# Half-filled key chunk of the expert attention on all 128 partitions, zeros laid by VectorE, and a new order of TensorE's work

## The chip, the cores and the metric

The kernel runs on one core of one Trainium2 chip. The core has TensorE (PE, with its weight loads shown apart as PEld), VectorE (DVE), ScalarE (ACT), GpSimd (POOL) and SyncE (SP), which here issues all the transfers. The metric is the device time of one execution in microseconds. Before the change the median of 3 runs is 1217.35 us (1216.65 to 1217.42).

## The reference, cut to what matters

Two layers follow each other. The first is attention of 8 batches with 8 heads each: queries are pooled in pairs (1152 become 576), keys and values stay 1152 long.

```python
q_pool = q.reshape(B, H, S // factor, factor, D).mean(axis=3)
scores = scale * np.matmul(q_pool, k.transpose(0, 1, 3, 2))
attn = np.exp(scores - max); attn = attn / (attn.sum(-1) + 1e-09)
attn_out = np.matmul(attn, v)                    # 8 x 8 x 576 x 64
```

The second is a layer of 4 experts over the 576 rows of each batch (512 wide). Each expert is a causal attention with a head of 64; a gate picks two experts for each row and weighs them.

```python
logits = x @ w_gate; topk = the 2 largest; w = softmax over the 2
for e in range(E):
    q, k, v = x @ wq[e], x @ wk[e], x @ wv[e]
    scores = np.where(causal, -1000000000.0, scale * (q @ k.transpose(0, 2, 1)))
    a = softmax(scores); ye = a @ v @ wo[e]
    out += (rows that chose e) * w * ye
```

## The kernel before

**Tiles.** Two heads of the first layer make a pair, and there are 32 pairs (4 in each batch). Scores are kept transposed, keys on partitions and queries in columns, in chunks of 128 keys; the 576 queries are cut into a block of 256 and one of 320. For each chunk PE makes the scores of both heads (line 325, three products of split operands and one that adds the row maximum), ACT turns them into exponentials in a tile `pt` of 128 x 2 x 320 (line 666), PE multiplies `pt` by the values into an accumulator (line 332, `pt,v`), and POOL adds `pt` onto a running sum `sacc` (line 349). At the end of a block PE multiplies `sacc` by ones (line 332, `sacc,ones`) to get the denominators, and DVE and ACT normalise. Row maxima come from separate products of queries and keys (line 325, `kh,qh`), which DVE reduces (line 572, `PM`).

**The experts.** After the four pairs of a batch, the expert layer of that batch runs in the same way, two experts at a time (`ep` 0 and 1), while the pairs of the next batch go on beside it. Its 576 keys make four chunks of 128 and one of 64. Chunk 4, the half chunk, meets only the last 64 queries of the block of 320. In it the scores, the exponentials (line 996), the causal mask by POOL (line 1014, an affine select) and POOL's sum (line 1046 by way of line 349) cover partitions 0 to 63 of a tile with 128. There are 16 half chunks (8 batches, 2 values of `ep`), so 16 such masks and 16 such sums; 14 of the sums are on POOL and 2, in the last batch, on DVE.

**Values of the experts.** They lie in `v32` (128 x 5 x 260); before the values of a batch are written, partitions 64 to 127 of its fifth part are set to zero by POOL (line 845), 8 times in all.

**What sets the order.** Nothing is scheduled at run time. The program is written by a planner: every piece of work is a flow that says when its inputs are ready by the planner's own clocks, and the loop at the end takes the best flow and writes its instructions to the engines' queues, which then run in that order. The flows have three modes by the shape in which PE's array is cut: A (64 rows by 128 columns, the scores), B (128 by 64, values and denominators) and C (128 by 128, projections and the rest). How long the planner stays in a mode, how many `pt` tiles it lets pile up and how it ranks row maxima and expert work is read from a table of 65 rows, one for each half of a pair: `HEAD` (16 rows), `CYCLE` (8 rows, used 5 times) and `TAIL` (9 rows). The five passes through `CYCLE` make the same order each time. The last batch of experts has nothing beside it and makes the end of the program.

A buffer is handed on through semaphores: who writes into a `pt` tile that was used before waits for the engines that read it last (PE and POOL).

Of the kernel before, what the change touches and what calls it, by code (L numbers as in the profile page):

```python
# [10 lines left out]
ALU = mybir.AluOpType  # L11
# [66 lines left out]
]  # L78
CYCLE = [
# [8 lines left out]
]  # L88
TAIL = [
# [71 lines left out]
def pooled_attention_then_moe_kernel(ctx: ExitStack, tc: tile.TileContext, qT, kT, vP, wall, wop, out):  # L161
    nc = tc.nc
# [146 lines left out]
    def pe_cost(n, m=128):  # L309
        return max(0.00086 * m, n * 0.000455 + 0.002)  # L310
# [24 lines left out]
    def act_copy(o, i, n, R, W, psum=True):  # L335
        nc.scalar.copy(o, i)  # L336
        emit("ACT", n / 1200 + (0.05 if psum else 0.083), R, W)
# [61 lines left out]
    def on(cond, *t):  # L399
        return max((0.0,) + t) if cond else INF  # L400
# [394 lines left out]
    def x_ready(b, halves):  # L795
        ps = range(b * NHP, b * NHP + NHP)
        if any(("x", p, h) not in flag for p in ps for h in halves):
            return INF
        return max(XR[p][h].rw for p in ps for h in halves)
# [37 lines left out]
    def f_vproj(b, pt):  # L837
        ts = ((0, 1), (2, 3, 4))[pt] if b == NB - 1 else range(5)
        for t in ts:
            n = min(128, SQ - 128 * t)  # L840
            hv = (0,) if t < 2 else (1,)
            yield (lambda: on("W" in flag, x_ready(b, hv), r_gen.avail(), r_v32.avail() if t == 0 else 0.0), "C")
            if t == 0:
                v32 = r_v32.new()
                nc.gpsimd.memset(v32[64:128, 4, :], 0.0)
                emit("POOL", 0.3, [], [v32])
                VG[b] = v32
            v32 = VG[b]
            ps = r_gen.new()
            xw(b, hv, ps[:n, :260], ps, lambda x, xi, W, hp: (x[:, xi, 128 * t:128 * t + n], W[:, hp, 512:772]),  # L850
               pe_cost(260))
            VT[b, t] = Res(None)
            act_copy(v32[:n, t, :], ps[:n, :260], 260, [ps], [v32, VT[b, t]])
            ps.free()
            flag.add(("v", b, t))
# [10 lines left out]
        ge, df, g, h = part(0, 16), part(16, 16), part(32, 4), part(36, 8)  # L866
        sq = lambda ap: ap.rearrange("p t (e f) -> p t e f", e=E)
        cm = [128, nt, E, E]

        def op(eng, f, *a, n=20, **kw):  # L870
# [34 lines left out]
           n=16 * nt)  # L905
# [62 lines left out]
    def f_mst(b, ep, pt):  # L968
        (qh, ql), (kh, kl) = MT[b, ep], MT[b, 2 + ep]
        rm = MRM[ep]  # L970
        tail = b == NB - 1
        for qb in ((pt,) if tail else (0, 1)):
            q0, qn = QB[qb]
            cl = (q0 + qn - 1) // 128

            span = lambda c: (max(0, 128 * c - q0), min(max(0, 128 * c - q0), qn - 128))
            for g in packed(range(cl + 1), lambda c: qn - span(c)[1]):
                yield (lambda: on(("mr", b, ep, pt) in flag and (("v", b, g[-1]) if tail else ("g", b, 0)) in flag
                                  and min(lows.get((b, m), 0) for m in (ep, 2 + ep)) > (pt if tail else 1),
                                  r_pt.avail(len(g)), r_gen.avail(2), kl.rw, ql.rw, rm.rw), "A")  # L980
                pts, st, o = [r_pt.new() for _ in g], [r_gen.new() for _ in range(2)], 0
                at = []
                for c in g:
                    kn, (f, w) = min(128, SQ - 128 * c), span(c)
                    kc, qc = slice(128 * c, 128 * c + kn), slice(q0 + w, q0 + qn)
                    rows2(lambda j: st[j][:kn, o:o + qn - w],
                          [(lambda r: kh[r, kc], lambda r: qh[r, qc]), (lambda r: kl[r, kc], lambda r: qh[r, qc]),
                           (lambda r: kh[r, kc], lambda r: ql[r, qc]), (lambda r: ON[r, :kn], lambda r: rm[r, qc])],
                          [kh, kl, qh, ql, rm], st)
                    o += qn - w  # L990
                    at.append(o)
                for j in range(2):
                    for c, pt_, o in zip(g, pts, at):
                        kn, f = min(128, SQ - 128 * c), span(c)[0]
                        n = qn - f
                        nc.scalar.activation(pt_[:kn, j, f:qn], st[j][:kn, o - n:o], AF.Exp, scale=0.125)
                        emit("ACT", n / 1200 + 0.06, [st[j]], [pt_], late=0.05)
                    st[j].free()
                for c, pt_ in zip(g, pts):
                    m_prog[b] += 0.48  # L1000
                    if 128 * c >= q0:
                        spawn("mask", f_mask(b, ep, qb, c, pt_, span(c)[0], min(128, SQ - 128 * c)))
                    else:
                        spawn("mav", f_mav(b, ep, qb, c, pt_), av_prio)
        if q0 + qn == SQ:
            flag.add(("mst", b, ep))
            for m in (ep, 2 + ep):
                for t in MT.pop((b, m)):
                    t.free()

    def f_mask(b, ep, qb, c, pt, f, kn):
        yield lambda: pt.rw
        sq = pt[:kn, :, f:f + kn]
        nc.gpsimd.affine_select(out=sq, in_=sq, compare_op=ALU.is_ge, fill=0.0, base=0,  # L1014
                                pattern=[[0, 2], [1, kn]], channel_multiplier=-1)
        emit("POOL", 0.15 + 0.0025 * kn, [pt], [pt])
        spawn("mav", f_mav(b, ep, qb, c, pt), av_prio)

    def f_mav(b, ep, qb, c, pt):
        q0, qn = QB[qb]  # L1020
        kn = min(128, SQ - 128 * c)
        f = max(0, 128 * c - q0)
        cl = (q0 + qn - 1) // 128
        v32, vr = VG[b], VT[b, c]
# [8 lines left out]
        acc, sacc = ACC[key], SACC[key]  # L1033
        n = qn - f
# [3 lines left out]
        if c == 0:  # L1038
            act_first(sacc[:, :, :qn], pt[:, :, :qn], 2 * qn, [pt], [sacc])
        else:  # L1040
            add = any_tt if tail_now() else pool_tt
            add(sacc[:kn, :, f:qn], sacc[:kn, :, f:qn], pt[:kn, :, f:qn], ALU.add, 2 * n, [pt], [sacc])
        pt.free()
        m_prog[b] += n * 0.0017
        if c == cl:
# [102 lines left out]
    while flows:  # L1148
# [16 lines left out]
        key, f, need = best  # L1165
# [31 lines left out]
```

## Time and profile before

| | |
|---|---|
| median of 3 runs | 1217.35 us |
| the profiled execution | 1215.55 us, of which its span 1213.8 us |
| PE busy | 1160.3 us (96% of the span) |
| POOL busy | 971.6 us (80%) |
| DVE busy | 877.6 us (72%) |
| ACT busy | 703.8 us (58%) |
| granted clock of TensorE | 0.996 |

The span runs from the first to the last instruction of the profiled execution; 1.75 us of its time lie outside it. Busy is the time in which an engine had an instruction under way; a PE that is shown busy is not always at its peak, since the ends of matmuls are modelled. A wait names the engine whose instruction came last before the waiting engine went on.

### The profile page before, as it was taken

How to read it: one execution, taken by the hardware profiler on the slowest of the kernel's cores; microseconds unless marked ns; L12 is line 12 of the kernel's file. 1: busy time of each engine (PE TensorE's matmuls, PEld its weight loads, DVE VectorE, ACT ScalarE, POOL GpSimd, SP SyncE). 2: the span in 40 equal slices, each digit the busy share in tenths (PEclk: the TensorE clock that was granted, in tenths of full speed). 3: DMA queues.
4: the chain of work that ended last, by engine and by line, in shares of the span. 5: the costliest groups of instructions: out<-in, count | busy, mean ns of one | idle time of the engine just before them, and what ended most of it. 6: DMA issues, size and time to landing. Idle time of an engine off the chain costs nothing.

```text
span 1213.8 us, 29441 instructions
## 1 busy us (share of the span) xinstructions
PE 1160.3 (96%) x11233; PEld 893.0 (74%) x11233; DVE 877.6 (72%) x2091; ACT 703.8 (58%) x2036; POOL 971.6 (80%) x850
## 2 busy tenths in 40 slices
PE   6999999999999999989999999998999989999998
PEld 5676786778767787667786677876877668877785
DVE  7897668776777857777677876777767876677265
ACT  5676446665466564665556654566546666465634
POOL 4999979887699866998669887698786986879921
PEclk9999999999999999999999999999999999999999
DMA  4232212031112211122011221112211122110001
GB/s 156 80 101 69 60 53 67 10 106 41 60 53 63 78 49 41 54 68 93 22 41 54 83 85 37 32 47 84 77 41 34 53 71 87 42 33 9 1 36 44
DMA packets 40425, 70.30 MB, mean 58 GB/s; under 512 B 4870, under 2 KB 31452, under 8 KB 40284
## 3 DMA queue, kind: packets, MB, share of 16 engines
q1 hardware_dynamic: 40284, 68.43, 18.2%
q8 instruction: 88, 1.44, 0.5%
q14 instruction: 53, 0.43, 0.1%
HBM read 58.73 MB, written 9.44 MB: 56 GB/s over the span
## 4 chain that ended last, share of the span: by engine, by line
PE 57%; POOL 29%; DVE 8%; issue 2%; ACT 2%; DMA 0%; POOLq 0%; SPq 0%; DVEq 0%; ACTq 0%
POOL sacc L349 25%; PE gen L325 23%; PE gen L316 17%; PE gen L332 16%; DVE qraw L345 3%; POOL kl L349 3%; POOL pt L1014 2%; DVE PM L572 1%; DVE gen L956 1%; ACT pt L666 1%; DVE ql L345 1%; PE gen L622 0%; DMA qraw<-in_qT 0%; DVE gen L734 0%; DVE gen L345 0%
## 5 line engine op out<-in xcount | busy, mean ns | idle before, releaser
L349 POOL TENSOR_TENSOR sacc<-sacc,pt 128x640 f32<-128x640 f32 (+4 forms) x586 | 824.8, 1412 | 138.2 <-ACT sacc L341 101.8
L572 DVE TENSOR_REDUCE PM<-gen 128x1 f32<-128x384 f32 x864 | 426.1, 550 | 164.1 <-PE gen L325 132.9
L666 ACT ACTIVATE pt<-gen 128x320 f32<-128x320 f32 (+1 forms) x1152 | 381.5, 433 | 142.9 <-PE gen L325 133.3
L332 PE MATMUL gen<-pt,v 128*64 128x320 f32 (+4 forms) x2752 | 354.8, 401 | 1.2
L332 PEld LDWEIGHTS gen<-pt,v 128*64 128x64 f32 (+1 forms) x2752 | 191.7, 137 | 136.8 <-issue 11.3
L325 PE MATMUL gen<-qh,kh 64*128 64x320 f32 (+1 forms) x1152 | 211.4, 317 | 13.4 <-DVE PM L572 10.9
L325 PE MATMUL gen<-qh,kl 64*128 64x320 f32 (+1 forms) x1152 | 196.0, 297 | 0.0
L325 PE MATMUL gen<-RM,ON 64*128 64x320 f32 (+1 forms) x1152 | 191.9, 293 | 0.8 <-ACT RM L336 0.8
L325 PE MATMUL gen<-ql,kh 64*128 64x320 f32 (+1 forms) x1152 | 191.3, 293 | 0.0
L325 PEld LDWEIGHTS gen<-qh,kh 64*128 64x128 f32 x1152 | 132.7, 186 | 45.8 <-DVE PM L572 18.6
L325 PE MATMUL gen<-kh,qh 64*128 64x384 f32 x768 | 156.8, 369 | 7.8 <-ACT qh L336 6.9
L325 PEld LDWEIGHTS gen<-RM,ON 64*128 64x128 f32 x1152 | 130.4, 187 | 1.2 <-ACT RM L336 1.0
L325 PEld LDWEIGHTS gen<-ql,kh 64*128 64x128 f32 x1152 | 129.7, 187 | 0.0
L325 PEld LDWEIGHTS gen<-qh,kl 64*128 64x128 f32 x1152 | 127.4, 187 | 0.0
L325 PEld LDWEIGHTS gen<-kh,qh 64*128 64x128 f32 x768 | 88.3, 188 | 38.5 <-issue 17.6
L316 PE MATMUL gen<-x,WH 128*128 128x320 f32 (+1 forms) x512 | 104.9, 299 | 6.8 <-DVE x L345 6.8
L349 POOL TENSOR_TENSOR kl<-kraw,kh 128x384 fp32r<-128x384 f32 x96 | 96.1, 1019 | 10.2 <-ACT mqh L336 5.2
L956 DVE CUSTOM_DVE_ANT_0 gen<-gen,mqk 64x288 f32<-64x288 f32 (+4 forms) x160 | 74.5, 504 | 23.8 <-PE gen L325 21.3
L316 PEld LDWEIGHTS gen<-x,WH 128*128 128x128 f32 x512 | 82.1, 188 | 10.0 <-issue 8.1
L332 PE MATMUL gen<-sacc,ones 128*64 128x320 f32 (+1 forms) x384 | 66.7, 428 | 14.5 <-POOL sacc L349 14.0
L316 PE MATMUL gen<-x,WL 128*128 128x320 f32 (+1 forms) x256 | 75.5, 295 | 0.0
L722 DVE STREAM_TRANSPOSE rd<-gen 128x256 f32<-128x256 f32 (+1 forms) x96 | 45.6, 475 | 41.3 <-PE gen L332 40.8
(115 smaller groups left out, 1575.6 us busy)
## 6 DMA issues: line engine op xcount, KB each, us to landing
kraw<-in_kT SPq DMA_DIRECT2D x96, 192.0 KB
v<-in_vP SPq DMA_DIRECT2D x96, 192.0 KB
qraw<-in_qT SPq DMA_DIRECT2D x31, 576.0 KB
out<-ob SPq DMA_DIRECT2D x28, 256.0 KB
wst<-in_wall SPq DMA_DIRECT2D x8, 193.0 KB
out<-pt SPq DMA_DIRECT2D x4, 256.0 KB
RM<-nt SPq DMA_DIRECT2D x62, 2.5 KB
out<-ob SPq DMA_DIRECT2D x6, 128.0 KB
```

The source lines that it names most:

```text
L316: nc.tensor.matmul(o, lhsT, rhs, start=start, stop=stop)
L325: nc.tensor.matmul(o(j), l(HEAD[j]), r(HEAD[j]), start=i == 0, stop=i == len(terms) - 1)
L332: nc.tensor.matmul(o(HEAD[j]), l(j), r(j), start=start, stop=stop)
L345: nc.vector.tensor_tensor(o, a, b, op=op)
L349: nc.gpsimd.tensor_tensor(o, a, b, op=op)
L572: nc.vector.tensor_reduce(pm[:, i, t:t + 1], ps[:, :384], axis=AX.X, op=ALU.max)
L666: nc.scalar.activation(pts[i][:, j, :qn], st[j][:, qn * i:qn * i + qn], AF.Exp, scale=0.0625)
L722: nc.vector.transpose(rd[:, :n], den[:, :n])
L956: nc.vector.tensor_tensor_reduce(p, p, mqk[:m, 384 + m - w:384 + m], 1.0, LOW, ALU.add, ALU.max, pm[:m, j, c, i:i + 1])
L1014: nc.gpsimd.affine_select(out=sq, in_=sq, compare_op=ALU.is_ge, fill=0.0, base=0, pattern=[[0, 2], [1, kn]], channel_multiplier=-1)
```

## The change

Three things are edited.

- The mask of a half chunk and the sum of every chunk name all 128 partitions. For the half chunk, VectorE first sets partitions 64 to 127 of the 64 columns to zero; this memset is written to its queue when the scores of the group are, before ScalarE's exponentials.
- The memset of `v32` goes from POOL to VectorE.
- In the planner's table four rows of `HEAD` and one of `TAIL` have other numbers. The order comes out otherwise in four places of PE's queue, and the same everywhere else: about 116 to 134 us, 188 to 294 us, 1030 to 1053 us and 1177 us to the end by the times of the profile before. Between 294 and 1030 us the queues of PE, ACT and SP are the same instruction by instruction, and those of POOL and DVE are the same apart from the first two edits. PE has the same matmuls before and after; it changes its mode 329 times before and 322 times after, 3 fewer between 188 and 294 us and 4 fewer behind 1177 us.

```diff
-    (0.2, 0.1, 0.2, 1, 4, 0.7, 0.12, 0.02, 2, 4.5, 3.9, 4.05, 4.1),
+    (0.2, 0.1, 0.2, 1, 4, 0.7, 0.25, 0.02, 2, 4.5, 3.9, 4.05, 4.75),
...
         if t == 0:
             v32 = r_v32.new()
-            nc.gpsimd.memset(v32[64:128, 4, :], 0.0)
-            emit("POOL", 0.3, [], [v32])
+            nc.vector.memset(v32[64:128, 4, :], 0.0)
+            emit("DVE", 0.3, [], [v32])
...
             pts, st, o = [r_pt.new() for _ in g], [r_gen.new() for _ in range(2)], 0
+            if g[-1] == 4:
+                nc.vector.memset(pts[-1][64:128, :, qn - 64:qn], 0.0)
+                emit("DVE", 0.13, [], [pts[-1]])
...
 def f_mask(b, ep, qb, c, pt, f, kn):
     yield lambda: pt.rw
-    sq = pt[:kn, :, f:f + kn]
+
+    sq = pt[:, :, f:f + kn]
...
-        add(sacc[:kn, :, f:qn], sacc[:kn, :, f:qn], pt[:kn, :, f:qn], ALU.add, 2 * n, [pt], [sacc])
+        add(sacc[:, :, f:qn], sacc[:, :, f:qn], pt[:, :, f:qn], ALU.add, 2 * n, [pt], [sacc])
```

DVE's queue in the first pass through `CYCLE`, at about 347 us (`ql` is the low part of a pair's queries, the ISA rows are the experts' row maxima). Before:

```order
L572 TENSOR_REDUCE PM_99<-gen_5614 128x1
L345 TENSOR_TENSOR ql_5632<-qraw_5042,qh_5109 128x576
L956 ISA gen_5686,MPM_103<-gen_5686,mqk 128x512
L956 ISA MPM_103 128x1
L956 ISA gen_5687,MPM_103<-gen_5687,mqk 128x512
```

The same place after:

```order
L572 TENSOR_REDUCE PM_99<-gen_5616 128x1
L345 TENSOR_TENSOR ql_5634<-qraw_5044,qh_5111 128x576
L983 MEMSET pt_5675 64x2x64
L956 ISA gen_5689,MPM_103<-gen_5689,mqk 128x512
L956 ISA MPM_103 128x1
```

One memset has come in between the subtraction and the row maxima; it waits for POOL's sum that read this `pt` tile last.

PE's queue at the end of the program, around the last denominators (`sacc,ones` is the denominators of the last block, `OH` and `OL` the output weights, `y_18932` or `y_18935` the first and `y_19049` or `y_19090` the second pair of experts). Before:

```order
L316 MATMUL gen_18989<-OH,y_19049 128x512 x2
L316 MATMUL gen_18989<-OL,y_19049 128x512
L332 MATMUL gen_19095<-pt_19115,v_8_18720 64x320 x2
L332 MATMUL gen_19095<-pt_19116,v_8_18720 64x192 x2
L332 MATMUL gen_19095<-pt_19152,v_8_18720 64x64 x2
L316 MATMUL gen_19186<-OH,y_18932 128x512 x2
L316 MATMUL gen_19186<-OL,y_18932 128x512
L316 MATMUL gen_19186<-OH,y_19049 128x512 x2
L316 MATMUL gen_19186<-OL,y_19049 128x512
L332 MATMUL gen_19198<-sacc_19096,ones 64x320 x2
L316 MATMUL gen_19202<-OH,y_18932 128x512 x2
L316 MATMUL gen_19202<-OL,y_18932 128x512
```

The same place after:

```order
L332 MATMUL gen_19109<-pt_19120,v_8_18734 64x320 x2
L332 MATMUL gen_19109<-pt_19121,v_8_18734 64x192 x2
L332 MATMUL gen_19109<-pt_19155,v_8_18734 64x64 x2
L316 MATMUL gen_19188<-OH,y_18935 128x512 x2
L316 MATMUL gen_19188<-OL,y_18935 128x512
L316 MATMUL gen_19188<-OH,y_19090 128x512 x2
L316 MATMUL gen_19188<-OL,y_19090 128x512
L316 MATMUL gen_19202<-OH,y_18935 128x512 x2
L316 MATMUL gen_19202<-OL,y_18935 128x512
L332 MATMUL gen_19207<-sacc_19110,ones 64x320 x2
L316 MATMUL gen_19202<-OH,y_19090 128x512 x2
L316 MATMUL gen_19202<-OL,y_19090 128x512
```

There are ten output products (an `OH` row and an `OL` row) in the queue's end. Before, four stand ahead of the last denominators (one of them further up) and six behind; after, three stand ahead and seven behind. The last three, which need what comes of these denominators, are the end of the queue in both. On DVE's queue the last whole chunk's addition to these denominators' `sacc` (line 345, 128 x 640) stands ahead of three instructions that normalise the block before (lines 731, 734 and 345), and before the change behind them.

PE's queue in the first expert layer, at about 189 us, where the row maxima of the experts (`mkh,mqh`) end. Before:

```order
L325 MATMUL gen_3038<-mkh_2179,mqh_2161 64x288
L316 MATMUL gen_3045<-kh_2580,QD_101 128x384
L316 MATMUL gen_3048<-kh_2732,QD_101 128x384
L622 MATMUL gen_3051<-ident,nm_3012 9x128
L332 MATMUL gen_3055<-sacc_2735,ones 64x256 x2
L332 MATMUL gen_3064<-pt_2961,v_2086 64x320 x2
```

What stands there after:

```order
L325 MATMUL gen_3159<-mkh_2432,mqh_2415 64x288
L622 MATMUL gen_3168<-ident,nm_3012 9x128
L622 MATMUL gen_3174<-ident,nm_3132 10x128
L316 MATMUL gen_3179<-gate_2864,rep 128x80
L332 MATMUL gen_3183<-sacc_2735,ones 64x256 x2
L332 MATMUL gen_3192<-pt_2961,v_2098 64x320 x2
```

The transposes (`ident`) and the gate product, which lay in two mode changes, lie in one, and the row maxima of the second pair of experts come ahead of them; behind the denominators nine products of `pt` follow without a break, where there were four.

## Rows read from the trace of the kernel before

**Rows 1.** The page: busy time and share of the span, by engine.

```profile
PE 1160.3 (96%) x11233; PEld 893.0 (74%) x11233; DVE 877.6 (72%) x2091; ACT 703.8 (58%) x2036; POOL 971.6 (80%) x850
```

**Rows 2.** Windows: stretch, length, busy us of PE, PEld, DVE, ACT, POOL; clock, DMA.

```profile
116.00:134.00 18.00, 16.59 (x169) 12.26 (x166) 11.84 (x26) 9.87 (x31) 17.14 (x13) 1.00 0.22 68
188.00:294.00 106.00, 105.09 (x1050) 79.25 (x1046) 80.23 (x190) 67.14 (x196) 91.00 (x79) 1.00 0.19 62
294.00:1030.00 736.00, 707.18 (x6944) 547.42 (x6944) 539.89 (x1255) 432.58 (x1255) 602.51 (x527) 1.00 0.19 58
1177.00:1213.80 36.80, 31.63 (x251) 21.14 (x249) 23.46 (x88) 17.36 (x52) 7.14 (x14) 0.97 0.11 37
```

**Rows 3.** Waits of PE, 294 to 1030 us: total, times, longest.

```profile
PE gen L325 <- DVE PM L572: 10.9, 5, 2.2
PE gen L332 <- POOL sacc L349: 7.2, 10, 1.0
```

**Rows 4.** Timeline of DVE, places of the first cycle and the last sum.

```profile
349.20 0.70 DVE L956 CUSTOM_DVE_ANT_0 gen<-gen,mqk 128x512 f32<-128x512 f32 x1 [0.88 <-PE gen L325]
...
382.37 0.56 DVE L572 TENSOR_REDUCE PM<-gen 128x1 f32<-128x384 f32 x1 [1.01 <-PE gen L316]
...
389.42 6.74 DVE L345 TENSOR_TENSOR qraw<-qraw 128x576 f32<-128x576 f32 x1
...
1202.41 0.28 DVE L345 TENSOR_TENSOR sacc<-sacc,pt 64x128 f32<-64x128 f32 x1 [1.19 <-POOL sacc L349]
```

**Rows 5.** Groups by shape, POOL: count, busy us, mean ns, idle before.

```profile
L1014 POOL TENSOR_SCALAR_AFFINE_SELECT pt<-pt 128x256 f32<-128x256 f32 x64 | 25.4, 418 | 32.6 <-ACT pt L996 32.6
L349 POOL TENSOR_TENSOR sacc<-sacc,pt 128x384 f32<-128x384 f32 x16 | 16.0, 998 | 3.5 <-DVE sacc L345 3.0
L349 POOL TENSOR_TENSOR sacc<-sacc,pt 128x256 f32<-128x256 f32 x16 | 12.2, 766 | 3.6 <-ACT sacc L341 3.6
L349 POOL TENSOR_TENSOR sacc<-sacc,pt 64x128 f32<-64x128 f32 x14 | 8.3, 593 | 0.9
L1014 POOL TENSOR_SCALAR_AFFINE_SELECT pt<-pt 64x128 f32<-64x128 f32 x16 | 7.3, 454 | 0.2 <-ACT pt L996 0.2
L845 POOL MEMSET v<- 64x260 f32 x8 | 2.5, 310 | 0.5
L172 POOL TENSOR_SCALAR_AFFINE_SELECT ident<-ident 128x128 f32<-128x128 f32 x1 | 0.3, 292 | 0.0
```

**Rows 6.** Line 1014 alone: shortest, median and longest ns, first and last start.

```profile
L1014 POOL TENSOR_SCALAR_AFFINE_SELECT pt<-pt x80: 285/406/936, 205.9 to 1199.7; 128x256 f32<-128x256 f32 x64, 64x128 f32<-64x128 f32 x16
```

**Rows 7.** Timeline of POOL: start, us, instructions, idle before and releaser.

```profile
360.98 0.46 POOL L349 TENSOR_TENSOR sacc<-sacc,pt 64x128 f32<-64x128 f32 x1
395.63 0.85 POOL L349 TENSOR_TENSOR sacc<-sacc,pt 64x128 f32<-64x128 f32 x1
...
437.53 3.98 POOL L349 TENSOR_TENSOR sacc<-sacc,pt 128x512 f32<-128x512 f32 x3 [9.16 <-ACT sacc L341]
```

**Rows 8.** Timeline of DVE at the program's start: a memset.

```profile
1.19 0.17 DVE L196 MEMSET ON<- 128x128 f32 x1
```

**Rows 9.** Timeline of PE, the last denominators and output products.

```profile
1202.99 0.76 PE L332 MATMUL gen<-sacc,ones 128*64 128x320 f32 x4
1203.68 0.73 PE L316 MATMUL gen<-OH,y 128*128 128x512 f32 x2
1204.25 0.40 PE L316 MATMUL gen<-OL,y 128*128 128x512 f32 x1
1204.48 0.63 PE L316 MATMUL gen<-OH,y 128*128 128x512 f32 x2
1204.95 0.40 PE L316 MATMUL gen<-OL,y 128*128 128x512 f32 x1
...
1206.45 1.07 PE L316 MATMUL gen<-OH,y 128*128 128x512 f32 x2 [0.40 <-ACT y L336]
```

**Rows 10.** Timeline of PEld: the same denominators' weights.

```profile
1202.99 0.20 PEld L332 LDWEIGHTS gen<-sacc,ones 128*64 128x64 f32 x4 [0.37 <-DVE sacc L345]
```

8 rows, old and new, of tables (HEAD, TAIL) are left out of this document.

## The prediction

> **What bounds the kernel now.** I read the page's busy line first [rows 1]: PE is busy 96% of the span, POOL 80%, DVE 72%. The reader is to see that about 53 us of PE's span are idle, and that a faster POOL or DVE pays only where PE waits for it. Then I read the busy time by stretches, cut where PE's queue differs between the two programs [rows 2]. From 294 to 1030 us, where PE, ACT and SP have the same instructions in the same order, PE has 736.00 - 707.18 = 28.8 us idle, 5.8 in each of five cycles. Between 188 and 294 us it has 0.9 idle, and behind 1177 us 5.2.
>
> Then the waits of PE in the five cycles [rows 3]: 10.9 us in five waits for DVE's `PM` and 7.2 us in ten waits for POOL's sum at the denominators. The first kind is one place in each cycle. DVE's subtraction `qraw`, which reads two operands, lasts 6.74 us there [rows 4], though 128x576 elements take a small part of that when nothing holds it, and the row maxima queue behind it. Neither edit touches that subtraction. So the bulk of the span repeats unless the edits move POOL or DVE at these waits.
>
> **The wider mask and sum.** The groups by shape [rows 5] seem to promise something. The half chunk's mask takes 454 ns on 64x128, a mask of 128x256 takes 418 and one of 128x128 (`ident`, line 172) 292. The sum takes 593 ns on 64x128; from 766 at 256 columns and 998 at 384 a sum of 128 columns would take 766 - 232 = 534. If the excess were the price of half the partitions, widening would save 16 x 0.162 + 14 x 0.059 = 3.4 us of POOL's time.
>
> The single rows say otherwise. The shortest mask of line 1014 took 285 ns [rows 6], and as none of 256 columns would be shorter than `ident`'s 292, it is one of the 64-partition ones. Two sums of one shape in one cycle took 0.46 and 0.85 us [rows 7], and the long one, at 395.63, starts while the `qraw` subtraction (389.42 + 6.74 = 396.16) is under way [rows 4]. The means are thus raised by a few instructions that stand beside a DVE instruction with two operands, and width is not the cause. I take 0 for the widening, between bounds of 3.4 us of POOL's time saved and, if a sum on all partitions were as long as the longer of the two sums, 14 x 0.39 = 5.5 us more. Even a gain would reach PE only through the ten waits for `sacc`, two in a cycle.
>
> On this the Trainium skill (GPSIMD Engine Reference, section 2 Architecture) says that each of the eight cores works on its own 16 partitions, which would leave four of them without work in a 64-partition instruction and its time unchanged; by that the saving is 0, and the single rows agree while the means do not.
>
> **The memset of v32.** POOL loses 8 x 0.31 = 2.5 us [rows 5]. In the cycles that relieves nothing: POOL sits idle 9.16 us before the sum at 437.53 [rows 7]. Taken 0; at best the 2.5 us come back.
>
> **The memsets on DVE.** There are 16 of 128 columns on 64 partitions; the nearest row, 128x128, took 0.17 us [rows 8], so 2.7 us together. The eight of `v32` (260 columns) are by size 0.17 x 260/128 = 0.35 us each, 2.8 together. Cover: they fall at places where DVE waited for PE's products anyway, 0.88 us before the row maxima at 349.20 and 1.01 before `PM` at 382.37 [rows 4]. Taken 0; all uncovered they are 5.5 us. The first adds a wait, since the memset needs a `pt` tile that POOL's sum has read. Behind it on DVE stand the experts' row maxima, for which ACT and then PE wait; but POOL's sums run earlier there than DVE arrives, by the slack that these gaps show.
>
> A memset on DVE could also be held by POOL, as `qraw` was. The Trainium skill (SBUF — State Buffer, section "Who interferes with whom") states that a DVE instruction contends with GpSimd when it reads two operands from SBUF or runs in a 2-port mode, and that whoever issues first keeps the shared ports. By it the memset, which reads nothing, is not held unless it runs in such a mode, and the sum stays as it is; the 6.74 us row agrees with the rule, and no row here shows a DVE memset beside a POOL sum.
>
> **The order of PE's work.** Between 188 and 294 us there are three mode changes fewer. A change costs little: at the end an `OH` product that follows the denominators starts its `OL` 0.57 us later (1203.68 to 1204.25), and one that follows its own kind 0.47 (1204.48 to 1204.95) [rows 9], so about 0.1 in the first product, and as much again, estimated, in leaving the old mode. 3 x 0.2 = 0.6 us. Upper bound: all of the 0.9 us idle on top, 1.5. Below nothing: new waits, rival three.
>
> In 116 to 134 us POOL is busy 17.14 of 18.00 and PE 16.59 [rows 2]; POOL paces it and its work is the same. 0, with bounds of 0.5 us either way. Between 1030 and 1053 us, where PE has the same products in another order, the same.
>
> At the tail, four mode changes fewer. Before, the last denominators start at 1202.99 and the first product that needs them at 1206.45, 3.46 us later, after 0.40 us of PE idle [rows 9]. That chain runs through DVE and ACT and is fixed. Three products filled it; after the change four do, each about 1204.48 - 1203.68 = 0.8 us at most. With one product fewer ahead of the denominators they come about 0.7 us earlier and the 0.40 us of idle closes. Against it: their weights already waited 0.37 us for DVE's sum [rows 10], and that sum (1202.41) had waited 1.19 us for POOL's [rows 4]. If the sums stayed there, the earlier denominators would gain nothing. But DVE's whole-chunk sum, for which POOL's waits, now stands ahead of three normalising instructions, so I let the sums come earlier by as much as the denominators. Taken: 0.7 for the denominators and 0.3 for what is left of the mode changes, -1.0 us. Bounds: +0.5 (the sums late) to -2.5 (all of the waits at 1202.99 to 1206.45 and four changes gone together).
>
> **The sum.** Widening 0, `v32` 0, memsets on DVE 0, mode changes -0.6, the two short stretches 0, tail -1.0: -1.6 us. The profiled execution took 1215.55 us, so 1213.95 for one like it. It lay 1.80 us under the median, which gives 1217.35 - 1.6 = 1215.75, say 1215.8. A measurement of this kernel can tell about 0.2%, 2.4 us, from no change: below 1214.9 is faster, above 1219.8 slower. The forecast is no measurable change.
>
> **Rivals.**
>
> One, POOL does get faster by the widening (means, not single rows). For: 454 against 292 ns [rows 5]. Against: 285 [rows 6]. Of the 3.4 + 2.5 us that POOL would save, the `sacc` waits could return 2.5 on top of the forecast: 1217.35 - 1.6 - 2.5 = 1213.3.
>
> Two, the order is worth more: the 0.9 us idle between 188 and 294 goes with the mode changes (-1.5), and behind 1177 us, where PE idles 5.2 us [rows 2], two more of the small waits close (-2.0). -3.5 gives 1213.8. For: the tail is a chain of short dependent steps, and moving a sum ahead of three instructions shortens each link behind it. Against: the last 3.46 us are fixed.
>
> Three, slower: in 188 to 294 us nine products of `pt` now follow the denominators without a break, so PE uses up its tiles faster than POOL, busy 91.0 of 106 us there [rows 2], adds them, and later denominators wait for the sum. The price is the longest such wait, 1.0 us [rows 3], at each. Up to four of them are eaten by the other gains (4.0 - 1.6 = 2.4); five and more decide: six give 1217.35 - 1.6 + 6.0 = 1221.8. Against: PE has 0.9 us idle there, and the stretch ends with the same queue as before.
>
> Four, slower: POOL's sums hold the DVE memsets. One of 998 ns [rows 5] makes a memset 1.17 us, 0.29 beyond the 0.88 of cover; at 16 places 4.6 us, so 1220.4. It decides when the holding exceeds the cover by 0.25 us at each. For: `qraw`'s 6.74 us [rows 4]; against: that one reads two operands.
>
> **How the numbers follow.** Forecast 0.48, rival one 0.08, two 0.25, three 0.12, four 0.07. Of the forecast's own range, 1214.7 to 1217.5, a small part (0.03) lies under 1214.9. Faster is 0.08 + 0.25 + 0.03 = 0.36, slower 0.12 + 0.07 = 0.19, the same 0.45. The range runs from 1212.6, under rivals one and two by the spread of the runs, to 1219.8: it leaves out the slower cases and a small part of the faster ones.
>
> **What would show it.** Right: the five cycles keep their length; POOL's masks and sums on 128 partitions have shortest rows of 0.29 and 0.46; the memsets on DVE take 0.17 and 0.35 with shorter idle ahead of what follows; the stretch that now ends at 294 us is 0.6 shorter; the last products follow the denominators with no idle. Wrong: cycles that change by over 0.3 us each, waits of PE for `sacc` in 188 to 294, memsets of 1 us, or denominators at the end that wait for DVE longer than 0.37.

## The result, and the profile after

The changed kernel takes 1204.42 us (median of 4 runs, 1204.27 to 1205.93) beside 1217.0 us of the kernel before (4 runs, 1215.95 to 1217.42): a ratio of 0.9901, 95% interval 0.9884 to 0.9918. It is 12.6 us faster, where 1.6 were forecast and the range ended at 1212.6.

The page of the changed kernel, busy time by engine. DVE's is 17 us shorter than before [rows 1], although DVE has 22 instructions more.

```profile
PE 1158.4 (96%) x11233; PEld 892.0 (74%) x11233; DVE 860.6 (71%) x2113; ACT 704.5 (58%) x2036; POOL 972.0 (81%) x844
```

The windows of the three long stretches, cut at the places that answer to 188 to 294, 294 to 1030 and 1177 us to the end of before (columns as in [rows 2]).

```profile
187.20:297.20 110.00, 108.23 (x1051) 80.13 (x1049) 80.22 (x194) 67.65 (x196) 91.20 (x79) 0.97 0.19 60
297.20:1019.00 721.80, 703.44 (x6948) 545.75 (x6946) 522.07 (x1270) 432.67 (x1255) 601.59 (x521) 1.00 0.20 59
...
1166.30:1204.20 37.90, 30.97 (x251) 21.34 (x247) 23.02 (x90) 17.05 (x52) 9.69 (x16) 0.98 0.11 36
```

The five cycles, where PE, ACT and SP have the same instructions in the same order, became 14.2 us shorter (736.0 to 721.8), of which 10.5 us are idle time of PE (28.8 to 18.4); the other 3.7 are busy time of PE, nearly all of it a lower clock before, as the end of this section shows. Both long stretches with a new order became longer, by 4.0 and 1.1 us (2.3 of the 4.0 are a lower clock in this one execution, shown below). So the sign of each was the other way than forecast: what was to stay gained, and what was to gain lost. Of the two short stretches, the one around 116 to 134 us became 1.4 us shorter and the one around 1030 to 1053 us 0.5 longer.

The waits of PE in the cycles (total, times, longest). The five waits for DVE's `PM`, 10.9 us [rows 3], are gone; the ten for POOL's sum are as they were.

```profile
PE gen L332 <- POOL sacc L349: 7.2, 10, 1.0
```

Behind that wait stood the `qraw` instruction of 6.74 us [rows 4] (the prediction calls it a subtraction; it adds the two halves of the pooled queries). First POOL's timeline in the kernel before around it: the mask of the half chunk on 64 partitions, and directly behind it a train, five of POOL's instructions that follow each other without a pause. The fifth ends at 394.55 + 1.00 = 395.55. Up to its next sum, at 395.63 [rows 7], POOL pauses for 0.08 us, and there DVE gets through.

```profile
388.75 0.31 POOL L1014 TENSOR_SCALAR_AFFINE_SELECT pt<-pt 64x128 f32<-64x128 f32 x1
389.01 4.63 POOL L349 TENSOR_TENSOR sacc<-sacc,pt 128x640 f32<-128x640 f32 x3
393.59 1.01 POOL L349 TENSOR_TENSOR kl<-kraw,kh 128x384 fp32r<-128x384 f32 x1
394.55 1.00 POOL L349 TENSOR_TENSOR sacc<-sacc,pt 128x384 f32<-128x384 f32 x1
```

The same place in the changed kernel, POOL (the mask is on 128 partitions now) and DVE. DVE gets through at the first boundary of two sums: it needs 1.79 us, and three sums take 5.15 instead of 4.63, because the second waits for it. Each of the five cycles shows 1.79 or 1.80 where it had 6.74 or 6.75.

```profile
392.00 0.29 POOL L1018 TENSOR_SCALAR_AFFINE_SELECT pt<-pt 128x128 f32<-128x128 f32 x1
392.26 5.15 POOL L349 TENSOR_TENSOR sacc<-sacc,pt 128x640 f32<-128x640 f32 x3
...
392.65 1.79 DVE L345 TENSOR_TENSOR qraw<-qraw 128x576 f32<-128x576 f32 x1
```

The groups that answer to [rows 5] and to the new memsets (count, busy, mean ns, idle before). The wide mask takes what the narrow one took (455 against 454); the sum's mean fell from 593 to 457, since none is held by the late DVE instruction any more. The memsets take 165 and 275 ns.

```profile
L1018 POOL TENSOR_SCALAR_AFFINE_SELECT pt<-pt 128x128 f32<-128x128 f32 x16 | 7.3, 455 | 0.2 <-ACT pt L999 0.2
L349 POOL TENSOR_TENSOR sacc<-sacc,pt 128x128 f32<-128x128 f32 x15 | 6.9, 457 | 0.9
L983 DVE MEMSET pt<- 64x128 f32 x16 | 2.6, 165 | 1.3
L845 DVE MEMSET v<- 64x260 f32 x8 | 2.2, 275 | 0.9
```

The stalls of `qraw` had a second price before. PE waits 2.2 us behind each of the five. Behind the second one (that wait ends at 545.41) the clock was granted at 0.50, its lower level of 1.2 GHz, for 3.4 us, and so it was behind the fourth; behind the other three it stayed at its upper level. Two windows of the kernel before (the clock is the third number from the right), then its first and second cycle from one `qraw` to the next, and the same two of the changed kernel, where the clock stays up:

```profile
544.00:546.00 2.00, 0.59 (x10) 0.59 (x12) 2.00 (x4) 1.08 (x3) 1.11 (x2) 1.00 0.00 0
546.20:549.70 3.50, 3.50 (x26) 2.24 (x22) 1.99 (x5) 2.72 (x9) 0.27 (x1) 0.51 0.45 140
389.42:538.15 148.73, 142.87 (x1410) 110.68 (x1410) 109.79 (x255) 87.39 (x254) 121.58 (x107) 1.00 0.19 58
538.15:686.85 148.70, 143.24 (x1404) 110.58 (x1404) 109.29 (x255) 86.91 (x253) 121.44 (x107) 0.99 0.18 56
```

```profile
392.65:539.20 146.55, 142.62 (x1411) 110.57 (x1410) 105.64 (x257) 87.67 (x254) 121.49 (x106) 1.00 0.20 59
539.20:684.04 144.84, 141.53 (x1404) 109.75 (x1404) 106.94 (x258) 86.80 (x253) 121.37 (x106) 1.00 0.19 58
```

The first gained 2.2 us, the second 3.9, of which 1.7 are busy time of PE. Two such drops of the clock make 3.4 of the 3.7 us above.

### The profile page after: what moved, and what is told of

Same layout as the page of the kernel before. It is cut to its first block, busy times and chain, and to the rows that moved or that the text cites. A ratio compares the mean times of both kernels' runs of the same rounds, so it can differ in the third digit from the quotient of the medians.

```text
span 1204.2 us, 29456 instructions
## 1 busy us (share of the span) xinstructions
PE 1158.4 (96%) x11233; PEld 892.0 (74%) x11233; DVE 860.6 (71%) x2113; ACT 704.5 (58%) x2036; POOL 972.0 (81%) x844
## 4 chain that ended last, share of the span: by engine, by line
PE 61%; POOL 27%; DVE 5%; ACT 3%; issue 3%; DMA 1%; POOLq 0%; SPq 0%; DVEq 0%; ACTq 0%
PE gen L325 24%; POOL sacc L349 23%; PE gen L316 19%; PE gen L332 17%; POOL kl L349 3%; ACT pt L666 2%; POOL pt L1018 1%; DVE gen L956 1%; DVE PM L572 1%; DVE ql L345 1%; ACT pt L999 1%; PE gen L622 0%; DVE gen L734 0%; DMA qraw<-in_qT 0%; DVE gen L345 0%
## 5 line engine op out<-in xcount | busy, mean ns | idle before, releaser
L336 ACT CAST x<-gen 128x256 fp32r<-128x256 f32 x64 | 25.8, 403 | 86.9 <-DVE gen L345 86.8
```

## The experiments

The theory formed from the two traces: a POOL instruction on fewer than 128 partitions, directly ahead of a train of sums, keeps DVE's two-operand instruction out until the train ends; the new order, which moves the instant at which DVE meets the train, and the memset of `v32` are the rivals. Five of the kernels below (m3, m2, m1b, m6 and m8) were timed in one execution each, and there it is the durations of `qraw`, cycle by cycle, that count.

**Which edit.** Four kernels, timed together with before (1216.92 us in these rounds). The first (e1) has the order of before on every engine:

```diff
+                if g[-1] == 4:
+                    nc.vector.memset(pts[-1][64:128, :, qn - 64:qn], 0.0)
...
-        sq = pt[:kn, :, f:f + kn]
+        sq = pt[:, :, f:f + kn]
...
-            add(sacc[:kn, :, f:qn], sacc[:kn, :, f:qn], pt[:kn, :, f:qn], ALU.add, ...)
+            add(sacc[:, :, f:qn], sacc[:, :, f:qn], pt[:, :, f:qn], ALU.add, ...)
```

Expected: 

> The order of before on every engine, with the mask and the sum of the half chunk on 128 partitions and the zeros laid by DVE (v32's memset stays on POOL). Theory 1 (width: an instruction on 64 partitions leaves POOL's cores out of step, so that the ports they share with DVE are never all free between back-to-back sums): the five qraw subtractions of 6.74 us shrink to about 1.8 and the time falls by 5 x 2.2 to 5 x 2.9 us, to 1202 to 1206. Theory 2 (the new order between 188 and 294 us shifts the phase at which DVE meets POOL): the 6.74 us stay, 1216 to 1218. Theory 3 (v32's memset off POOL does it): 1216 to 1218 as well.

Measured: 1201.69 us, ratio 0.9875 (0.9858 to 0.9891), all five at 1.80 or 1.81 us. The width alone gains 15.2 us; neither the order nor `v32` is needed, and with them the kernel is 2.7 us slower than with the width alone.

The other three keep the changed kernel's order and go back to 64 partitions in both (e2), in the mask alone (e3), in the sum alone (e4):

```diff
-        sq = pt[:, :, f:f + kn]
+        sq = pt[:kn, :, f:f + kn]
...
-            add(sacc[:, :, f:qn], sacc[:, :, f:qn], pt[:, :, f:qn], ALU.add, ...)
+            add(sacc[:kn, :, f:qn], sacc[:kn, :, f:qn], pt[:kn, :, f:qn], ALU.add, ...)
```

Expected of both narrow: 

> The changed kernel, its order on every engine kept, with mask and sum back on 64 partitions (the zeros are still laid). Theory 1: the 6.74 us stalls are back in each cycle and the time is 1215 to 1220, since the order of 188 to 294 us and the tail cost what the two traces showed (+3.9 and +1.1 us). Theories 2 and 3: no stall, 1203 to 1206.

Expected of the mask alone: 

> The changed kernel with the mask alone back on 64 partitions, the sum on 128. In the trace of before the narrow mask stands directly ahead of the train of sums in which DVE was held, the narrow sum at its end. Theory 1 with the mask as the cause: stalls of about 6 us are back, 1215 to 1220. If the sum is the cause, or the phase: 1203 to 1206.

Expected of the sum alone: 

> The changed kernel with the sum alone back on 64 partitions, the mask on 128. Theory 1 with the mask as the cause: no stall over 2.1 us in DVE's qraw, 1203 to 1206. If the narrow sum is the cause: 1215 to 1220.

Measured: 1220.83 us (ratio 1.0029, 1.0016 to 1.0042), 1220.48 us (1.0026, 1.0015 to 1.0037) and 1204.42 us (0.9898, 0.9883 to 0.9912). The first two have five stalls of 6.74 to 6.77 us, the third none over 1.83. The mask's width is worth 16 us, the sum's nothing. Part of the 16 is the clock: in the profiled execution of e3 it fell to 0.50 behind three of the five stalls. With both back on 64 partitions the change is a loss of 3.9 us. Over all the kernels here, the clock fell within the five cycles behind 16 of 27 stalls of `qraw`, for 3.4 us each, and never in the seven kernels that have no stall.

**Is it the instant?** Before, with one to five DVE memsets ahead of the held instruction (m3):

```diff
+        if p in LAG:                      # {13: 1, 17: 2, 21: 3, 25: 4, 29: 5}
+            for _ in range(LAG[p]):
+                nc.vector.memset(SCR[:, :], 0.0)
         any_tt(q[:, 0, :], q[:, 0, :], q[:, 1, :], ALU.add, SQ, [q], [q])
```

Expected: 

> Before, with 1 to 5 memsets on DVE (256 columns, about 0.3 us each) ahead of the held qraw subtraction in the first to fifth cycle, so that it comes at five other phases of POOL's sums. Theory 1 (no gap in the whole train): it ends at the same place in each cycle, at the end of the train, so it takes about 6.4, 6.1, 5.8, 5.5 and 5.2 us, and the time stays at 1215 to 1218. Theory 2 (phase): it is under 2.5 us in some of the cycles.

Measured: 6.47, 6.11, 5.68, 5.30 and 4.93 us, 1216.96 us in all. Whenever it comes, it is held to the end of the train. DVE in the first and the fifth cycle:

```profile
389.39 6.47 DVE L347 TENSOR_TENSOR qraw<-qraw 128x576 f32<-128x576 f32 x1
...
987.51 4.93 DVE L347 TENSOR_TENSOR qraw<-qraw 128x576 f32<-128x576 f32 x1
```

**How narrow?** e1, with another width of the mask in each cycle (m2):

```diff
-        sq = pt[:, :, f:f + kn]
+        sq = pt[:kn if kn == 128 else {1: 64, 2: 80, 3: 96, 4: 112}.get(b, 128), :, f:f + kn]
```

Expected: 

> The order of before with the sum on 128 partitions and the mask of the half chunk on 64, 80, 96, 112 and 128 in the first to fifth cycle. Theory 1a: any core left out of the mask runs ahead, so qraw takes 5 to 7 us in cycles 1 to 4 and 1.8 us in the fifth. If only a split in two halves matters: 6.7 us in the first cycle alone. Phase (theory 2): no rule in the widths. With 4 stalls of 5 the time is about 1214, with one about 1205.

Measured: 6.75, 6.75, 6.76, 6.77 and 1.80 us, and 1213.99 us. Sixteen partitions left out do as much as 64. The fourth cycle (its narrow mask and DVE's wait) and DVE in the fifth:

```profile
834.83 0.31 POOL L1016 TENSOR_SCALAR_AFFINE_SELECT pt<-pt 112x128 f32<-112x128 f32 x1
835.50 6.77 DVE L345 TENSOR_TENSOR qraw<-qraw 128x576 f32<-128x576 f32 x1
...
984.20 1.80 DVE L345 TENSOR_TENSOR qraw<-qraw 128x576 f32<-128x576 f32 x1
```

**Why does a narrow one do it?** The guess was that the part of POOL without work runs ahead and stays ahead. The first trial (m1) adds a second narrow mask on the upper half behind the lower one, in the kernel before:

```diff
+        if kn < 128:
+            up, src = pt[kn:2 * kn, :, f:f + kn], ident[kn:2 * kn, :].rearrange("p (j c) -> p j c", j=2)
+            nc.gpsimd.affine_select(out=up, in_=src, compare_op=ALU.is_ge, fill=0.0, base=0,
+                                    pattern=[[0, 2], [1, kn]], channel_multiplier=-1)
```

Expected: 

> Before, with a second narrow mask instruction behind each narrow one, on partitions 64 to 127 of the same columns (nobody reads what it writes there; no zeros on DVE, sum on 64). Theory 1a (the narrow instruction lets the idle cores of POOL run ahead, and they stay ahead through the back-to-back sums): the second one lets the other half catch up, the five stalls of 6.74 us go and the time is 1201 to 1206. Theory 1b (each instruction on fewer partitions does the harm by itself, in whatever pair): the stalls stay, 1216 to 1220.

Measured: 1203.70 us, ratio 0.9894 (0.9879 to 0.9909). The stalls are gone, but `qraw` takes 0.75 us, so DVE did not come in within the train but before it, in a pause of 0.08 us that POOL made between the second mask and the first sum. I took the pause for a wait of the second mask for the first and tried to remove the wait, by letting it write a scratch tile (m1b, `up` in `SCR`):

Expected: 

> m1 again without its gap: in m1 the second narrow mask waited for the first, POOL had a pause of 0.08 us before the sums, and DVE's qraw got in there (0.75 us), before the train. Here the second one writes a scratch tile that nothing else uses, so it waits for nothing and the sums follow at once. Theory 1a (cores out of step; the second lets the others catch up): DVE comes in at the first boundary of two sums as in the changed kernel, 1.7 to 2.3 us in all five cycles, and the time is 1202 to 1205. Theory 1b (a narrow instruction does harm by itself): 6.7 us, 1216 to 1219. If the two halves are only nearly in step, values between.

Measured: 1203.02 us and again 0.74 or 0.75 us. The pauses are still there, 0.06 us ahead of the upper mask and 0.09 us behind it:

```profile
388.15 0.65 POOL L1015 TENSOR_SCALAR_AFFINE_SELECT pt<-pt 128x256 f32<-128x256 f32 x2
388.86 0.29 POOL L1019 TENSOR_SCALAR_AFFINE_SELECT SCR<-ident 64x128 f32<-64x128 f32 x1
389.16 0.74 DVE L346 TENSOR_TENSOR qraw<-qraw 128x576 f32<-128x576 f32 x1
389.24 2.09 POOL L350 TENSOR_TENSOR sacc<-sacc,pt 128x640 f32<-128x640 f32 x1
```

The scratch tile did not remove the wait. In the records of this trace the upper mask, and the sum behind it, wait for the semaphore that POOL's own instructions raise; the lower mask, which follows without a pause, does not. In the kernel before the same wait stands at 470 of the 472 instructions that POOL starts after a pause of 0.04 to 0.10 us. So the pauses are POOL waiting for its own earlier instruction, as the program has it; why it has it at these two, the runs do not show. This pair shows that a pause of under 0.1 us is enough to let DVE in; whether the halves catch up it cannot tell. Two more kernels (m6 and m8) put small memsets of a scratch tile between the wide mask and the train, another kind in each cycle (the second is the same with other entries):

```diff
+EXTRA = {1: [(0, 64, 8)], 2: [(0, 64, 64)], 3: [(0, 64, 256)], 4: [(0, 128, 64)], 5: [(0, 64, 64), (64, 128, 64)]}
...
+        if kn < 128 and ep == 1:
+            for lo, hi, n in EXTRA.get(b, ()):
+                nc.gpsimd.memset(SCR[lo:hi, :n], 0.0)
```

Expected of the first: 

> The order of before with mask and sum on 128 partitions (no stall in e1), and one more POOL memset of a scratch tile between the wide mask and the train of sums: 64 partitions x 8 columns in the first cycle, x 64 in the second, x 256 in the third, 128 partitions x 64 in the fourth, and 64 columns on the lower and then the upper 64 partitions in the fifth. Theory 1a: qraw takes over 5 us in cycles 1 to 3 (in the first perhaps less, if so small a lead is lost again), 1.8 in cycles 4 and 5. Theory 1b: over 5 us in 1, 2, 3 and 5. If it is the mask and not the width: 1.8 us in all. With three stalls the time is about 1211, with none 1203.

Expected of the second: 

> As m6 (wide mask and sum, one more POOL memset of a scratch tile ahead of the train), to see what the lead is made of: cycle 1 the upper 64 partitions x 64 columns alone, cycle 2 four memsets of 64 partitions x 8 columns (m6 had one, 0.10 us, and no stall), cycle 3 64 x 32, cycle 4 64 x 64 followed by one of 128 x 64, cycle 5 four of 128 x 8. Theory 1a (idle cores run ahead and keep the lead): cycle 1 stalls for 6 to 7 us as the lower half does, cycle 2 stalls (four small leads add up), cycle 3 stalls or not by where the threshold lies between 8 and 64 columns, cycle 4 stalls (a wide one behind does not give the lead back), cycle 5 has 1.8 us. If only the instruction directly ahead of the first sum counts: no stall in cycle 4, and none in cycle 2.

Measured, first kernel (1210.34 us): 1.84, 6.83, 7.02, 1.90 and 0.75 us. The memset and `qraw` in the first, second and fourth cycle:

```profile
389.68 0.10 POOL L1022 MEMSET SCR<- 64x8 f32 x1
390.10 1.84 DVE L347 TENSOR_TENSOR qraw<-qraw 128x576 f32<-128x576 f32 x1
...
535.96 0.14 POOL L1022 MEMSET SCR<- 64x64 f32 x1
536.38 6.83 DVE L347 TENSOR_TENSOR qraw<-qraw 128x576 f32<-128x576 f32 x1
...
835.22 0.17 POOL L1022 MEMSET SCR<- 128x64 f32 x1
835.64 1.90 DVE L347 TENSOR_TENSOR qraw<-qraw 128x576 f32<-128x576 f32 x1
```

Second kernel (1204.66 us): 2.10, 1.93, 1.85, 6.91 and 1.96 us. Its first and fourth cycles (the last memset row holds two, 64 x 64 and behind it 128 x 64):

```profile
388.21 0.15 POOL L1023 MEMSET SCR<- 64x64 f32 x1
388.52 2.10 DVE L348 TENSOR_TENSOR qraw<-qraw 128x576 f32<-128x576 f32 x1
...
825.50 0.25 POOL L1023 MEMSET SCR<- 64x64 f32 x2
825.92 6.91 DVE L348 TENSOR_TENSOR qraw<-qraw 128x576 f32<-128x576 f32 x1
```

What follows: the operation does not matter (mask or memset), and the width does: 64 partitions x 64 columns stall, 128 x 64 do not. A wide one behind a narrow one does not undo it (fourth cycle here, the memset of 64 x 64 and one of 128 x 64). A narrow one must be long enough: 0.10 and 0.12 us (8 and 32 columns) did nothing, 0.14 us did, and four of 8 columns did not add up, against what I expected. The upper half alone stalled nothing (2.10 us), but POOL waited for itself on both sides of that memset (0.06 and 0.09 us), as it did around the upper one of the first kernel's fifth cycle and not around the lower ones. So the upper half is not decided: its waits may have undone what it did. Whether parts of POOL run ahead cannot be seen in the trace, which has one row for the whole engine; that stays a guess, and the four small memsets speak against its simple form.

**What the order costs.** A version that takes what gained (m5): e1, with only the first changed row of the table (it rewrites 116 to 134 us), and the last batch left on 64 partitions without zeros.

```diff
-    (0.2, 0.1, 0.2, 1, 4, 0.7, 0.12, 0.02, 2, 4.5, 3.9, 4.05, 4.1),
+    (0.2, 0.1, 0.2, 1, 4, 0.7, 0.25, 0.02, 2, 4.5, 3.9, 4.05, 4.75),
...
-                if g[-1] == 4:
+                if g[-1] == 4 and b < NB - 1:
...
-        sq = pt[:, :, f:f + kn]
+        sq = pt[:kn if b == NB - 1 else 128, :, f:f + kn]
```

Expected: 

> A version meant to beat both: the order of before with only the table's first changed row (116 to 134 us), mask and sum on 128 partitions with zeros by DVE in the first seven batches, both on 64 in the last batch, v32's memset on POOL. From e1 (1201.7): -1.3 for 116 to 134 us and -1.0 for the end, where e1 showed 0.6 us of PE idle that before did not have: 1199.4, between 1198.5 and 1201.7. If the last batch's width is not what costs at the end: 1200.4.

Measured: 1199.84 us (1199.71 to 1199.98), ratio 0.9862 (0.9845 to 0.9878). It beats both kernels, the changed one by 4.6 us. Then the three rows of 188 to 294 us were put into it (m7):

```diff
-    (0.05, 0.2, 0.3, 1, 3, 1.4, 0.2, -0.02, 3, 4.05, 2.9, 4.6, 4.75),
+    (0.15, 0.1, 0.3, 1, 4, 0.9, 0.3, -0.02, 0, 4.5, 3.9, 4.6, 4.55),
...
-    (0.2, 0.1, 0.6, 3, 1, 1.2, 0.12, -0.02, 2, 4.05, 3.9, 4.05, 4.55),
+    (0.2, 0.1, 0.3, 3, 2, 1.2, 0.12, -0.04, 2, 4.05, 3.9, 4.6, 4.55),
...
-    (0.05, 0.1, 0.1, 2, 1, 1.0, 0.16, 0.04, 1, 4.5, 3.9, 4.05, 4.1),
+    (0.05, 0.1, 0.1, 2, 1, 0.9, 0.12, 0.04, 1, 4.5, 3.9, 4.05, 4.1),
```

Expected: 

> m5 with the three changed rows of the table that rewrite 188 to 294 us, everything else as in m5. The trace of the changed kernel showed PE waiting 1.2 us there for DVE's row maxima of the experts, and this stretch 1.6 to 3.9 us longer than before. Theory: the order of this stretch costs 1.5 to 3 us, so 1201.3 to 1202.9 against 1199.84 for m5. If the order is worth the 0.6 us of the prediction: 1199.2.

Measured: 1202.76 us, ratio 0.9894 (0.9877 to 0.9911): 2.9 us lost by the order of this stretch. PE waits there 1.5 us for DVE, in three places, and once for ACT, which the changed kernel does not show (total, times, longest):

```profile
PE gen L316 <- ACT QD L336: 1.2, 1, 1.2
```

The timeline of the changed kernel shows where it waits for DVE: the transposes of the experts' row maxima and the gate product, which now stand together right behind the row maxima's products, wait for DVE, which is still reducing them.

```profile
194.97 0.28 PE L622 MATMUL gen<-ident,nm 128*9 128x128 f32 x1 [0.69 <-DVE MPM L956]
...
195.74 0.38 PE L622 MATMUL gen<-ident,nm 128*10 128x128 f32 x1 [0.50 <-DVE MPM L956]
...
196.35 0.69 PE L316 MATMUL gen<-gate,rep 128*128 128x80 f32 x2 [0.23 <-DVE MPM L956]
```

That pause had a second price in the profiled execution of the changed kernel. Its windows there (the clock is the third number from the right), and then those of the kernel with the narrow sum (e4), which has the same order and the same pause, with the whole stretch of 188 to 294 us as its last row:

```profile
194.00:196.00 2.00, 0.81 (x4) 0.23 (x3) 1.93 (x10) 1.32 (x3) 0.00 (x0) 0.90 0.56 172
196.00:200.00 4.00, 3.77 (x15) 1.99 (x16) 3.92 (x16) 0.28 (x1) 3.48 (x3) 0.50 0.00 0
200.00:204.00 4.00, 4.00 (x24) 1.99 (x22) 2.01 (x5) 0.37 (x1) 3.84 (x3) 0.70 0.28 59
```

```profile
194.00:196.00 2.00, 0.59 (x3) 0.24 (x3) 1.93 (x10) 1.16 (x3) 0.10 (x1) 1.00 0.38 113
196.00:200.00 4.00, 4.00 (x28) 2.06 (x30) 3.89 (x15) 0.00 (x0) 3.84 (x3) 1.00 0.00 1
186.90:294.60 107.70, 105.55 (x1051) 78.84 (x1048) 80.50 (x195) 67.58 (x195) 91.42 (x78) 1.00 0.19 61
```

In the first, after PE had been busy for 0.81 of 2 us, the clock was granted at 0.50, its lower level of 1.2 GHz, for 4 us and came back within the next 4; the stretch took 110.0 us. In the second, after 0.59 of 2 us, it stayed at its upper level, and the stretch took 107.7: 2.3 us of the changed kernel's 4.0 are the clock, and 1.7 the order. Of the five profiled executions with this order the clock fell at this pause in three (the changed kernel, e2, e3) and not in two (e4, m7), so the pause does not bring it about each time. The changed kernel's profiled execution took 1205.93 us and its three others 1204.27 to 1204.53.

## Why the prediction was wrong

**What bounds the kernel.** The reading was right: PE is the bound, and the largest of its repeated waits is the one for `PM` behind `qraw`. The step that failed is the one drawn from it, "Neither edit touches that subtraction", and with it "the bulk of the span repeats". The mask one instruction ahead of the train did touch it (e3 and e4: 1220.48 against 1204.42 us). I had named the 6.74 us as a case of two operands beside POOL and left it at that. The trace of before had more: 31 such `qraw` instructions, of which five took 6.74 or 6.75 us and no other more than 2.02. What those five had in front of them on POOL, a 64-partition mask directly ahead of the train, was the question to ask. The cycles, which were to keep their length, each became shorter by 2.1 us or more.

**The wider mask and sum.** The cost on POOL itself came out as taken: 455 ns for 454, and the two long kinds of row were indeed those beside a DVE instruction. But I bounded the edit by POOL's own time alone, between 3.4 us saved and 5.5 lost, and by what of it would reach PE through `sacc`. Its effect lay on another engine, and no bound covered it. The conclusion drawn beside the Trainium skill's rule (GPSIMD Engine Reference, section 2 Architecture: each core works on its own 16 partitions) was wrong in the same way: a narrow mask does take as long as a wide one (454 and 455 ns), and the edit was worth far more than the 0 that was concluded from it. The Trainium skill's rule in SBUF — State Buffer, section "Who interferes with whom", that whoever issues first gets the shared ports for the whole instruction, does not account for the five rows, although the prediction read them as agreeing with it: behind a narrow instruction DVE was kept out over five POOL instructions, 6.74 us, and only behind wide ones did it come in at the end of one.

**v32 and DVE's memsets.** Both taken at 0. The memsets took 165 and 275 ns (0.17 and 0.35 were taken); none was held (all 16 took 165 ns, all eight 275), so rival four fell. What the move of `v32` alone is worth was not tried.

**The order, 188 to 294 us.** Forecast -0.6, measured +2.9 (m7 against m5, 1.2 of it in the wait for ACT that only m7 has); by the trace of e4 +1.7, at the upper clock. The step that failed is pricing a regrouping by the mode changes it saves, without asking what the regrouped instructions wait for; the transposes that now stand first at that place need DVE's row maxima, which are produced just before. Rival three had the sign, at +2.4 and more, by another mechanism: PE waited for DVE, not for POOL's sums.

**116 to 134 us and the tail.** The first was put at 0, within 0.5 us either way, since POOL paced it. It gained 1.4 us. Between the same two products, before and after:

```profile
108.10:140.00 31.90, 29.14 (x274) 22.26 (x275) 18.73 (x41) 17.16 (x49) 30.59 (x23) 1.00 0.18 57
108.70:139.20 30.50, 28.66 (x274) 21.99 (x275) 19.47 (x41) 17.27 (x49) 29.32 (x22) 1.00 0.20 59
```

The reading that POOL's work there is the same did not hold for the time it takes: 1.3 us less of POOL's busy time falls into the stretch, and PE idles 0.9 us less. In the tail, the end came as described: three products, the denominators, and four products without idle.

```profile
1193.42 0.76 PE L332 MATMUL gen<-sacc,ones 128*64 128x320 f32 x4
...
1197.03 0.87 PE L316 MATMUL gen<-OH,y 128*128 128x512 f32 x2
```

From the denominators to the first product that needs them it is 3.61 us, against 3.46 [rows 9], and the 0.40 us of idle is closed. But PE's idle time in the stretch grew from 5.2 to 6.9 us, by new waits earlier in it (total, times, longest), so -1.0 became +1.1 in the traces. First the changed kernel's, then those of e1, which has the order of before, and e1's stretch:

```profile
PE gen L622 <- DVE nm L618: 1.2, 1, 1.2
PE gen L316 <- DVE MPM L956: 0.6, 1, 0.6
PE gen L332 <- POOL pt L1018: 0.5, 2, 0.3
```

```profile
PE gen L332 <- POOL pt L1016: 0.8, 2, 0.6
1162.70:1200.40 37.70, 31.66 (x249) 21.08 (x249) 23.82 (x88) 17.37 (x52) 7.79 (x14) 0.98 0.11 36
```

With the order of before, e1 is about 1 us longer there as well (37.7 against 36.8), with a wait for the wide mask, while m5, whose last batch is narrow and has no zeros, is as long as before (36.7 us). So the sum failed at two steps: the wide last batch was put at 0 for the tail and costs about 1 us with the order of before, and the gain of the new order was priced at the denominators alone, without the waits for DVE (1.2 and 0.6) that it brings earlier. The new order of the tail without the zeros was not tried, so the two shares of the +1.1 stay open.

**Together.** The width's -15.2 us (e1, which holds the price of the wide last batch) and the +2.9 of the order of 188 to 294 us leave -12.3 of the -12.6. That they nearly meet is in part luck: the -1.4 and +0.5 of the short stretches are not in this sum, and the clock fell in some of these executions and not in others. The forecast had the largest term at 0, missed the -1.4, and had 188 to 294 us and the tail with the wrong sign.

## What to carry to other kernels

Where a two-operand DVE instruction is many times longer than its like, look at what POOL ran directly ahead of it, not only beside it, and try POOL's instructions on all 128 partitions, even where half of them carry zeros. Leave them narrow where no DVE instruction is held: in the last batch the wide ones and their zeros cost about 1 us (e1 against m5). Price an edit by what it does to the engine that shares a port, not only by its own duration. Before counting the mode changes that a regrouping saves, look up who produces the inputs of each moved instruction, and when.

## What was not expected of the hardware

- A POOL mask on 64, 80, 96 or 112 partitions that begins at partition 0 (0.28 to 0.31 us), or a memset on 64 (0.14 us or more), ahead of a train of back-to-back sums, keeps a DVE addition of 128x576 (0.75 us when nothing holds it) waiting for the whole train, 6.7 to 7.0 us; with all of them on 128 partitions it waits for one boundary, 1.8 to 1.9 us.
- The state outlasts a wide POOL instruction (6.91 us in the fourth cycle of the second memset kernel), and 0.10 to 0.12 us of narrow work does not bring it about, nor four of 0.10 us.
- A pause of 0.08 us of POOL ahead of the train lets DVE in (0.74 or 0.75 us) even where a narrow mask stands ahead of it (m1 and m1b). POOL makes such pauses where an instruction waits for POOL's own earlier one.
- Behind 16 of the 27 stalls of `qraw` in the profiled executions the granted clock was 0.50 for 3.4 us, and it never fell within the five cycles of a kernel that has no stall. At PE's pause near 194 us, of 0.7 and 0.5 us with little work between, it fell in three of the five profiled executions with that order.
